# Parking weights in DRAM later, and counting their buffers by their last reader, in an attention + two-FFN kernel on one core

## The chip, the cores and the metric

One NeuronCore of a Trainium2 chip runs the whole program. The metric is the device time of one execution in microseconds; the figure for the kernel before is the median of three runs.

## The reference

Causal local/strided attention (4 batches, 8 heads, 576 positions, head size 64), then a gated feed-forward layer behind an RMS norm, then a second one without a norm. There are 2304 tokens, the model width is 512 and the hidden width 1536; all data are float32.

```python
attn = softmax(where(mask, q @ k.T / 8, -1e9))            # heads 0-3: local 32, heads 4-7: same position mod 32
x = (attn @ v).transpose(0, 2, 1, 3).reshape(2304, 512)
x = x / sqrt(mean(x * x) + 1e-6) * rms_g                  # first layer only
for w_gate, w_val, w_out in (layer1, layer2):
    g = x @ w_gate
    x = (g * sigmoid(g) * (x @ w_val)) @ w_out
```

## The kernel before, in words

**Arithmetic.** Each float32 operand is split in a high and a low part, and each product is made of three TensorE products (high·high, high·low, low·high). A weight comes from DRAM as words into a `raw` buffer (512 KB, `fetch`, L218). `scale` rebuilds it into `dh` in four operations: two on ScalarE (`low` L235, `high` L227), two on VectorE (`sign` L239, `join` L244). Then ScalarE casts the high part and VectorE subtracts it for the low part.

**Stages.** The hidden width is cut into 12 chunks of 128 columns per layer. Chunks 0 to 5 of the first layer are multiplied while attention still runs, in six token segments (`segs`, numbers 0 to 5) with `gate` and `down`. All other chunks go through the Strassen stage: 15 items (`work`), five passes of three token blocks of 768. The passes hold chunks (6, 7, 8) and (9, 10, 11) of the first layer, and (0..3), (4..7), (8..11) of the second. A chunk is seven products (steps 1 to 7) on `xq`, sums of quarters of x. GpSimd makes those: `sum_x` (L1165, on x fetched by `stage_x`, L1159) and the low parts `xl` in `split_q` (L1182). The next item's x is split while this item's last chunk is multiplied. `first_x` (L1064 to L1081) does the same for item 0 during segment 5, into the pool `x7`.

**Weights of the Strassen stage.** `combined_step` turns gate and value weight into seven quarter sums. Its operations in order: two loads, 4 + 4 of `scale`, one `sums` (four GpSimd subtractions, L326, VectorE's results in, VectorE's next inputs out), then a cast (L358) and a subtraction (L362) for each of four pieces. With "keep" (c) the pieces land in rooms of SBUF. With "park" (p) they overwrite `raw` and `dh`, and after each piece `save` stores the two halves to DRAM (`pk`, L370 and L371); `recall_step` (r, L397) later loads the four pieces into rooms with no arithmetic. `weight_step` (d) does a w_out chunk. Rooms: 20 of 4 KB and 5 of 2 KB per partition; a chunk of the Strassen stage takes 3 + 1, and one for w_out. A pass gives its rooms back chunk by chunk in its third item (`used`).

**The planner.** `plan` writes the order of these steps by hand into `late`. `point()` is called at fixed places between TensorE's products; each call advances `clock` by one, loads the next step of `late` if it is `ready`, and adds `pace["op"]` to an allowance from which operations of the steps begun are emitted. A step waits `state["wait"]` points after its load, and `state["lag"]` points before the operation marked `late`. `need_w` emits whatever is missing at a chunk's first use. A count `free` of raw buffers per rack (`racks[0]`) lets a step load: three in the pool `dec`, which also holds the x of the segments (`load_x`, L865), and five in the pool `st`. `st` is opened when attention is closed (L1107) and taken down at the start of segment 5, after `while begun: operate(begun[0])`.

**Order on the engines.** Each engine runs its queue in order, and the order is fixed at build time by priority: an instruction's place in the program, less an offset (`PRIO` 200 for path operations, `PRIO_W` -150 for the weights). `behind(eng)` puts a weight operation after the last path operation of its engine. All DMAs but two are issued by SyncE.

The lines that the change sits on, as they read before:

```python
            cell["bk"]["free"] += free                       # join: buffer counted free at once
        pace["op"] = 2.0                                     # segments
        state["lag"], state["wait"] = 10 if n else 5, 9      # items
            if z == 5 and nxt:
                cell = stage_x(nxt[0], nxt[2])
            if i == 0 and nxt:
                sum_x(cell)
```

Of the kernel before, what the change touches and what calls it, by code (L numbers as in the profile page):

```python
# [25 lines left out]
def attn_ffn_ffn(ctx: ExitStack, tc: tile.TileContext, q, k, v, w1g, w1v, w1o, rms_g, w2g, w2v, w2o, out):  # L26
# [117 lines left out]
    def weights():  # L144
        clock[0] += 1
        prefetch()
        have["op"] = min(have["op"] + pace["op"], 3.0)
        while have["op"] >= 1.0:
            fit = [st for st in begun if clock[0] - st.at >= st.lag]
            if not fit:  # L150
                break
            have["op"] -= 1.0
            operate(fit[0])
# [50 lines left out]

    rack = {"pool": dec, "free": 3, "bufs": 3, "dh": 2}
    racks = [rack]
    parked = {}
# [14 lines left out]
    def scale(cell, free=1):  # L222

        def high():
            cell["h"] = cell["bk"]["pool"].tile([128, 512], F32, tag="dh", name="dh", bufs=cell["bk"]["dh"])
            with behind("act"):
                nc.scalar.activation(out=cell["h"], in_=cell["hw"].bitcast(F32), func=AF.Copy, scale=2.0 ** -112)  # L227

        def low():
            cell["r"] = cell["lw"]  # L230
            if spare:
                spare.append(spare.pop(0))
                cell["r"] = pp.tile([128, 512], U32, tag=spare[-1], name="lws")
            with behind("act"):
                nc.scalar.activation(out=cell["r"], in_=cell["lw"], func=AF.Copy, scale=LOW)  # L235

        def sign():
            with behind("dve"):
                nc.vector.scalar_tensor_tensor(out=cell["r"], in0=cell["hw"], scalar=0x80000000, in1=cell["r"], op0=ALU.bitwise_and, op1=ALU.bitwise_or)  # L239

        def join():
            h = cell["h"].bitcast(U32)
            with behind("dve"):
                nc.vector.scalar_tensor_tensor(out=h, in0=h, scalar=3, in1=cell["r"], op0=ALU.logical_shift_left, op1=ALU.bitwise_or)  # L244
            cell["bk"]["free"] += free

        return [low, high, sign, join]

# [8 lines left out]
    def weight_step(m, c, z, park=False):  # L257
# [11 lines left out]
        def second():  # L269
            lo(cell["t"], cell["h"])  # L270
            wt[m, c, z] = cell["t"]
            wdone.add((m, c, z))
# [15 lines left out]
        def save():  # L288
            h, a = parts()
            d = dp.tile([128, 2, 512], F32, name=f"pk{m}_{c}")  # L290
            nc.sync.dma_start(out=d[:, 0], in_=h.bitcast(F32))
            nc.sync.dma_start(out=d[:, 1], in_=a)
            cell["bk"]["free"] += 1
            parked[m, c, z] = d

        return Step([load] + scale(cell, int(not park)) + ([high, low, save] if park else [first, second]),
                    lambda: (park or room[4]) and racks[0]["free"] >= 1, PRIO_W)

    QUARTERS = ((1, 2), (5, 6), (7, 4), (3,))

    def combined_step(m, c, how):
# [7 lines left out]
        def ready():  # L309
            if racks[0]["free"] < 2:  # L310
                return False
            return how == "park" or len(room[4]) >= n4 and len(room[2]) >= 7 - 2 * n4

# [6 lines left out]
        def sums():  # L320
# [3 lines left out]
            b12, b22 = v["h"][:, 0:256], v["h"][:, 256:512]  # L324
            for z, a, b in ((0, b12, b11), (2, b22, b12), (1, b22, t[:, 0]), (3, b21, t[:, 1])):
                nc.gpsimd.tensor_tensor(out=t[:, z], in0=a, in1=b, op=ALU.subtract)  # L326
            spaces = v["raw"].rearrange("p k f -> p (k f)").bitcast(F32)
# [16 lines left out]
        def op(i, f):  # L344
            def g_():
                f(*parts[i])
                if i == len(parts) - 1 and f is (save if how == "park" else second):
                    g["bk"]["free"] += 1
                    if how == "park":
                        v["bk"]["free"] += 1  # L350
                    else:
# [647 lines left out]
    def plan(text):  # L999
        for word in text.split():  # L1000
# [10 lines left out]

    plan("p19 p110 c16 d16 c17 c18 d17 d18 r19 d19 r110 d110 p111 p20 r111 d111 p21 r20 d20 r21 d21 p22 p23 r22 d22 r23 d23 "
         "c24 d24 p25 p26 p27 r25 d25 r26 d26 r27 d27 c28 d28 p29 p210 p211 r29 d29 r210 d210 r211 d211")
# [81 lines left out]
    for si, (m, t0, n, c0, c1) in enumerate(segs):  # L1095
# [10 lines left out]
        pace["dec"] = 0.25  # L1106
        pace["op"] = 2.0  # L1107
        xs = xs_of.pop(si)
        state["tanh"] = True and att is not None
        for c in range(c0, c1):  # L1110
# [6 lines left out]
            if att and not steps and not active_att():  # L1117
# [5 lines left out]
                open_pool("st", "st", 0, bufs=1)  # L1123
                racks.insert(0, {"pool": pools["st"][0], "free": 5, "bufs": 5, "dh": 5})
                room[4] += [(pools["wpb"][0], f"v{i}") for i in range(2)]
# [217 lines left out]
    for n, (m, cs, t0) in enumerate(work):  # L1343
# [51 lines left out]
        pace["op"] = 0.6 if n else 1.0  # L1395
        state["lag"], state["wait"] = 10 if n else 5, 9
        for z in (1, 0, 0, 2, 6, 0, 5, 7, 0):
            step(chunks[0], z) if z else blank()
            if z == 5 and nxt:
                cell = stage_x(nxt[0], nxt[2])  # L1400
            if z == 2:
                spare[:] = ya[halves[0].n:]
        for i, c in enumerate(chunks[:-1]):
# [6 lines left out]
            step(c1, 2)  # L1410
            if i == 0 and nxt:
                sum_x(cell)
            if i == k - 2:
                pace["op"] = 0.6 if n else 0.8
            step(c1, 6)
            blank()
# [59 lines left out]
```

## Time and profile before

| | us |
|---|---|
| median of 3 runs (lowest to highest) | 1059.54 (1057.32 to 1061.37) |
| the profiled execution's own time | 1058.73 |
| its span, first to last instruction | 1056.9 |
| TensorE busy / idle in the span | 992.2 / 64.7 |
| VectorE, ScalarE, GpSimd busy | 589.0, 575.5, 472.9 |
| DMA moved | 181.60 MB |
| mean granted TensorE clock (1.00 is full) | 0.964 |

Time runs from the span's start. A view of windows gives, for each stretch, its length, each engine's busy time with the number of instructions in brackets, the granted TensorE clock, the busy share of the DMA engines and what they moved. A row of waits names the engine and line that waited, what released it, and the total, the number of times and the longest, in us.

### The profile page before, as it was taken

The page shows a single profiled execution, that of the slowest core. Times are in us where ns is not written, and L with a number is a line of the kernel's source. Part 1 is how long each engine was busy: PE and PEld are TensorE (multiplying, and loading weights), DVE is VectorE, ACT ScalarE, POOL GpSimd, SP SyncE. Part 2 cuts the span into 40 slices and gives each one's busy share as a digit, 9 for nine tenths or more (in the row PEclk, how much of TensorE's full clock was granted, in tenths as well). Part 3 has the DMA queues.
Part 4 walks back from the last instruction along what each step waited for, and adds up shares of the span by engine and source line. Part 5 has one row for each costly group of instructions (what it writes and reads, how often), then busy time and mean ns, then how long its engine had stood idle before and what let it go on. Part 6 is the DMA issues. An engine that isn't in the chain of part 4 may idle for free. (4 is left out here: it accounts for less than half of the span.)

```text
span 1056.9 us, 16819 instructions
## 1 busy us (share of the span) xinstructions
PE 992.2 (94%) x5804; PEld 905.4 (86%) x5804; DVE 589.0 (56%) x1289; ACT 575.5 (54%) x1435; POOL 472.9 (45%) x485
## 2 busy tenths in 40 slices
PE   5758979999999997999987999999999999999998
PEld 4647869878778986999987999999998999899997
DVE  3779546445434186764756666555547665633433
ACT  5878745636633355753663565656547455643431
POOL 3312212203100294675956865837557473745500
PEclk9758989999999998999999999999999999999999
DMA  7576445224105129677687595257862739815021
GB/s 196 157 221 182 146 135 161 66 65 127 40 26 185 53 89 348 203 251 243 209 256 246 201 343 181 92 188 255 285 237 75 254 126 349 269 64 180 30 80 60
DMA packets 153277, 181.60 MB, mean 172 GB/s; under 512 B 44132, under 2 KB 120364, under 8 KB 153192
## 3 DMA queue, kind: packets, MB, share of 16 engines
q1 hardware_dynamic: 153000, 180.25, 52.6%
q8 instruction: 46, 0.75, 0.3%
q14 instruction: 39, 0.32, 0.1%
q0 software_dynamic: 192, 0.28, 0.1%
HBM read 123.60 MB, written 56.89 MB: 171 GB/s over the span
## 5 line engine op out<-in xcount | busy, mean ns | idle before, releaser
L1182 POOL TENSOR_TENSOR xl<-xst,xh 128x384 fp32r<-128x384 f32 x168 | 185.6, 1136 | 70.9 <-PE b_a L66 42.8
L66 PE MATMUL b_y<-xh,w 128*128 128x384 f32 x700 | 188.6, 336 | 4.0 <-ACT t L1210 4.0
L66 PE MATMUL b_g<-xh,w 128*128 128x384 f32 (+2 forms) x496 | 150.8, 352 | 9.7 <-ACT xh L905 7.0
L66 PEld LDWEIGHTS b_y<-xh,w 128*128 128x128 f32 x700 | 127.6, 188 | 7.6 <-ACT t L1210 5.7
L66 PE MATMUL b_a<-xh,w 128*128 128x384 f32 (+2 forms) x460 | 126.3, 338 | 5.6 <-DVE t L1220 5.5
L66 PE MATMUL b_v<-xh,w 128*128 128x384 f32 (+2 forms) x432 | 129.7, 350 | 0.0
L66 PE MATMUL b_y<-hh,w 128*128 128x256 f32 (+2 forms) x432 | 119.1, 347 | 3.7 <-ACT hh L892 3.7
L66 PE MATMUL b_y<-xl,w 128*128 128x384 f32 x350 | 117.4, 335 | 0.0
L66 PEld LDWEIGHTS b_g<-xh,w 128*128 128x128 f32 x496 | 93.3, 196 | 16.4 <-ACT xh L905 7.2
L66 PEld LDWEIGHTS b_a<-xh,w 128*128 128x128 f32 x460 | 83.9, 189 | 9.6 <-DVE t L1220 6.0
L635 POOL TENSOR_TENSOR e<-e,rc 128x384 f32<-128x384 f32 (+3 forms) x40 | 38.3, 961 | 119.6 <-DVE rc L629 84.3
L1181 ACT CAST xh<-xst 128x384 fp32r<-128x384 f32 x168 | 80.2, 522 | 12.5 <-POOL xst L1165 12.4
L66 PEld LDWEIGHTS b_y<-hh,w 128*128 128x128 f32 x432 | 78.3, 191 | 10.1 <-ACT hh L892 4.0
L66 PEld LDWEIGHTS b_v<-xh,w 128*128 128x128 f32 x432 | 79.7, 192 | 6.7 <-issue 0.4
L66 PE MATMUL b_g<-xl,w 128*128 128x384 f32 (+2 forms) x248 | 85.4, 344 | 0.0
L66 PE MATMUL b_a<-xl,w 128*128 128x384 f32 (+2 forms) x230 | 77.6, 337 | 0.0
L66 PE MATMUL b_y<-hl,w 128*128 128x256 f32 (+2 forms) x216 | 73.8, 342 | 2.4 <-DVE hl L893 1.7
L1165 POOL TENSOR_TENSOR s<-xst 128x384 f32<-128x384 f32 x28 | 28.8, 1049 | 104.5 <-DMA xst<-y_d 71.8
L66 PE MATMUL b_v<-xl,w 128*128 128x384 f32 (+2 forms) x216 | 73.5, 340 | 0.0
L66 PEld LDWEIGHTS b_y<-xl,w 128*128 128x128 f32 x350 | 65.7, 188 | 1.8
L66 PE MATMUL b_y<-w,hh 128*128 128x512 f32 x216 | 67.1, 392 | 0.0
L618 ACT ACTIVATE e<-e,nb 128x96 f32<-128x96 f32 (+2 forms) x152 | 56.6, 376 | 19.2 <-DVE nb L609 19.2
(210 smaller groups left out, 2198.3 us busy)
## 6 DMA issues: line engine op xcount, KB each, us to landing
w<-pk SPq DMA_DIRECT2D x39, 512.0 KB
pk<-raw SPq DMA_DIRECT2D x65, 256.0 KB
xst<-y_d SPq DMA_DIRECT2D x18, 768.0 KB
raw<-in_moe_w_gate_dram SPq DMA_DIRECT2D x24, 512.0 KB
raw<-in_moe_w_val_dram SPq DMA_DIRECT2D x24, 512.0 KB
raw<-in_moe_w_out_dram SPq DMA_DIRECT2D x24, 512.0 KB
part<-ob SPq DMA_DIRECT2D x48, 256.0 KB
ob<-part SPq DMA_DIRECT2D x36, 256.0 KB
```

The source lines that it names most:

```text
L66: traced(nc.tensor.matmul(out_, a, b_, start=start, stop=stop, **how))
L618: r = nc.scalar.activation(out=e[:qn, i, :kn], in_=e[:qn, i, :kn], func=AF.Exp, bias=nb[:qn, i:i + 1], scale=-1.0, accum_out=sums[:qn, i:i ...
L635: eng.tensor_tensor(out=e[:qn, :nt, :kn], in0=e[:qn, :nt, :kn], in1=rc[:qn, :nt].unsqueeze(2).to_broadcast([qn, nt, kn]), op=ALU.mult)
L1165: eng.tensor_tensor(out=out_[:, kk], in0=a[:, kk], in1=b[:, kk], op=op)
L1181: nc.scalar.copy(out=xh[:, kk], in_=src[:, kk])
L1182: eng.tensor_tensor(out=xl[:, kk], in0=src[:, kk], in1=xh[:, kk].bitcast(F32), op=ALU.subtract)
```

## The change

Parks start only once attention is over (`att is None`). The plan parks chunk 6 too and recalls it; chunk 11 of the first layer and chunks 0 and 1 of the second are no longer parked but split straight from their load, so 11 combined weights are parked in place of 13. A `raw` buffer is counted free six points after its last reader is emitted (`back`); each rack also counts its `dh` buffers (`words`, `spent`), and `high` (`cell`) is emitted only if one is free. `sums` is emitted with a priority offset of 200. `pace["op"]` is 2.5 in the segments before the last and 1.5 in the last; lag and wait become 6 and 6 in a segment that begins after attention, and 10 (8 in item 0) and 12 in the items. `stage_x` is emitted behind step 1 of an item's first chunk in place of step 5, and `sum_x` in loop k - 3 (the same loop for k = 3, one later for k = 4).

```diff
-            fit = [st for st in begun if clock[0] - st.at >= st.lag]
+            fit = [st for st in begun if clock[0] - st.at >= st.lag and (not hasattr(st[0], "cell") or words(st[0].cell["bk"]) > 0)]
...
-    rack = {"pool": dec, "free": 3, "bufs": 3, "dh": 2}
-    racks = [rack]
+    racks = [{"pool": dec, "free": 3, "bufs": 3, "dh": 2, "back": [], "words": 2, "wback": []}]
+
+    def back(bk, n):
+        bk["back"].append((clock[0] + 6, n))
+
+    def words(bk):
+        while bk["wback"] and bk["wback"][0] <= clock[0]:
+            bk["words"] += 1
+            bk["wback"].pop(0)
+        return bk["words"]
+
+    def spent(bk, n):
+        bk["wback"].append(clock[0] + n)
+        bk["wback"].sort()
+
+    def spaces():
+        bk = racks[0]
+        while bk["back"] and bk["back"][0][0] <= clock[0]:
+            bk["free"] += bk["back"].pop(0)[1]
+        return bk["free"]
...
         def high():
+            cell["bk"]["words"] -= 1
...
-            cell["bk"]["free"] += free
-
+            back(cell["bk"], free)
+
+        high.cell = cell
...
             lo(cell["t"], cell["h"])
+            spent(cell["bk"], 4)
...
-            cell["bk"]["free"] += 1
+            back(cell["bk"], 1)
+            spent(cell["bk"], 6)
...
-            if racks[0]["free"] < 2:
+            if spaces() < 2:
                 return False
-            return how == "park" or len(room[4]) >= n4 and len(room[2]) >= 7 - 2 * n4
+            return how == "park" and att is None or how != "park" and len(room[4]) >= n4 and len(room[2]) >= 7 - 2 * n4
...
-            for z, a, b in ((0, b12, b11), (2, b22, b12), (1, b22, t[:, 0]), (3, b21, t[:, 1])):
-                nc.gpsimd.tensor_tensor(out=t[:, z], in0=a, in1=b, op=ALU.subtract)
+            with tc.high_priority(offset=PRIO):
+                for z, a, b in ((0, b12, b11), (2, b22, b12), (1, b22, t[:, 0]), (3, b21, t[:, 1])):
+                    nc.gpsimd.tensor_tensor(out=t[:, z], in0=a, in1=b, op=ALU.subtract)
...
                 f(*parts[i])
+                if f is (save if how == "park" else second) and parts[i][0][0] in (1, 3):
+                    spent((g if parts[i][0][0] == 1 else v)["bk"], 6 if how == "park" else 8)
                 if i == len(parts) - 1 and f is (save if how == "park" else second):
-                    g["bk"]["free"] += 1
+                    back(g["bk"], 1)
                     if how == "park":
-                        v["bk"]["free"] += 1
+                        back(v["bk"], 1)
...
-    plan("p19 p110 c16 d16 c17 c18 d17 d18 r19 d19 r110 d110 p111 p20 r111 d111 p21 r20 d20 r21 d21 p22 p23 r22 d22 r23 d23 "
+    plan("p16 p19 p110 r16 d16 c17 c18 d17 d18 p22 r19 d19 r110 d110 p23 c111 d111 c20 d20 c21 d21 r22 d22 r23 d23 "
          "c24 d24 p25 p26 p27 r25 d25 r26 d26 r27 d27 c28 d28 p29 p210 p211 r29 d29 r210 d210 r211 d211")
...
-        pace["op"] = 2.0
+        pace["op"] = 2.5 if si < NA - 1 else 1.5
+        state["lag"], state["wait"] = (6, 6) if att is None else (3, 4)
...
-        state["lag"], state["wait"] = 10 if n else 5, 9
+        state["lag"], state["wait"] = 10 if n else 8, 12
         for z in (1, 0, 0, 2, 6, 0, 5, 7, 0):
             step(chunks[0], z) if z else blank()
-            if z == 5 and nxt:
+            if z == 1 and nxt:
                 cell = stage_x(nxt[0], nxt[2])
...
-            if i == 0 and nxt:
-                sum_x(cell)
             if i == k - 2:
                 pace["op"] = 0.6 if n else 0.8
+            if i == k - 3 and nxt:
+                sum_x(cell)
```

## Rows read from the trace of the kernel before

**Rows 1.** The page's 40 slices of the span: TensorE's busy tenths.
```profile
PE   5758979999999997999987999999999999999998
```

**Rows 2.** Windows of 5 us in the attention stage.
```profile
120.00:125.00 5.00, 2.87 (x18) 2.61 (x18) 2.82 (x14) 4.14 (x15) 0.26 (x1) 0.72 0.47 166
...
130.00:135.00 5.00, 1.93 (x18) 1.42 (x14) 4.50 (x12) 4.59 (x16) 4.04 (x5) 1.00 0.24 79
135.00:140.00 5.00, 1.03 (x3) 0.86 (x4) 2.33 (x8) 1.33 (x3) 0.78 (x1) 0.58 0.96 310
140.00:145.00 5.00, 5.00 (x44) 4.77 (x43) 1.84 (x4) 1.65 (x4) 0.00 (x0) 0.73 0.53 178
```

**Rows 3.** What ScalarE waited for, 100 to 145 us.
```profile
ACT xh L905 <- DMA xraw<-x_d: 3.9, 1, 3.9
ACT raw L358 <- DMA pk<-raw: 3.6, 1, 3.6
```

**Rows 4.** Timeline of SyncE's queue, 130 to 145 us (start, us, what).
```profile
134.07 0.38 SPq L865 DMA_DIRECT2D xraw<-x_d  x1
```

**Rows 5.** Windows of 5 us from the end of segment 5 on.
```profile
405.00:410.00 5.00, 1.98 (x11) 1.49 (x9) 1.49 (x3) 1.65 (x4) 4.84 (x6) 0.89 1.03 410
410.00:415.00 5.00, 2.67 (x6) 1.78 (x7) 4.97 (x7) 2.86 (x6) 1.92 (x2) 0.50 0.85 283
415.00:420.00 5.00, 5.00 (x17) 4.32 (x16) 3.58 (x6) 3.46 (x7) 0.00 (x0) 0.59 0.96 346
...
535.00:540.00 5.00, 2.08 (x12) 1.76 (x11) 0.65 (x1) 1.03 (x2) 3.87 (x4) 1.00 0.77 237
575.00:580.00 5.00, 0.45 (x3) 0.13 (x1) 1.03 (x1) 0.47 (x1) 3.68 (x5) 0.96 0.52 177
580.00:585.00 5.00, 4.04 (x13) 4.05 (x14) 3.15 (x7) 1.41 (x3) 3.31 (x3) 0.50 0.28 105
585.00:590.00 5.00, 5.00 (x27) 5.00 (x26) 2.78 (x4) 3.82 (x10) 3.18 (x3) 0.86 0.41 143
```

**Rows 6.** Waits of all engines, 405 to 420 us.
```profile
ACT raw L235 <- DMA raw<-in_moe_w_out_dram: 3.9, 1, 3.9
PE b_y L66 <- ACT hh L892: 3.7, 1, 3.7
```

**Rows 7.** Waits of all engines, 535 to 540 us.
```profile
ACT dh L227 <- DMA pk<-dh: 5.0, 1, 5.0
```

**Rows 8.** Waits of all engines, 565 to 590 us.
```profile
DVE dh L362 <- POOL raw L326: 8.3, 1, 8.3
POOL s L1165 <- DMA xst<-x_d: 6.6, 1, 6.6
```

**Rows 9.** Windows: segment 4, and segment 5.
```profile
326.00:357.00 31.00, 31.00 (x228) 29.60 (x227) 9.79 (x20) 10.01 (x20) 0.00 (x0) 1.00 0.36 117
357.00:405.00 48.00, 48.00 (x224) 40.20 (x223) 31.86 (x38) 26.59 (x52) 36.35 (x32) 1.00 0.41 130
```

**Rows 10.** Instruction groups by line (busy us, mean ns, idle before them).
```profile
L244 DVE SCALAR_TENSOR_TENSOR dh<-dh,raw 128x512 uint32<-128x512 uint32 x53 | 51.0, 963 | 10.7 <-ACT dh L227 9.7
L239 DVE SCALAR_TENSOR_TENSOR raw<-raw 128x512 uint32<-128x512 uint32 x53 | 47.5, 898 | 21.9 <-ACT raw L235 21.6
...
L362 DVE TENSOR_TENSOR raw<-raw 128x512 fp32r<-128x512 f32 x26 | 22.2, 858 | 8.8 <-ACT raw L358 8.6
...
L244 DVE SCALAR_TENSOR_TENSOR dh<-dh,lws 128x512 uint32<-128x512 uint32 x19 | 13.0, 684 | 1.0 <-ACT dh L227 0.4
...
L326 POOL TENSOR_TENSOR raw<-dh 128x256 f32<-128x256 f32 x36 | 28.5, 814 | 74.2 <-DVE dh L244 42.7 <-ACT b_v L1216 21.0 <-ACT w L358 7.5
```

**Rows 11.** The chain that ended last (start, us, what): two like places.
```profile
723.78 1.36 PE b_y L66 x6
...
816.08 1.36 PE b_y L66 x6
```

**Rows 12.** Waits of all engines, whole span.
```profile
POOL raw L326 <- DVE dh L244: 42.7, 10, 8.2
```

More of the change, by code (lines that the diff above doesn't have):

```diff
@@ L292, in save @@
             nc.sync.dma_start(out=d[:, 1], in_=a)
-            cell["bk"]["free"] += 1
+            back(cell["bk"], 1)
+            spent(cell["bk"], 6)
             parked[m, c, z] = d
         return Step([load] + scale(cell, int(not park)) + ([high, low, save] if park else [first, second]),
-                    lambda: (park or room[4]) and racks[0]["free"] >= 1, PRIO_W)
+                    lambda: (park or room[4]) and spaces() >= 1, PRIO_W)
     QUARTERS = ((1, 2), (5, 6), (7, 4), (3,))
@@ L1123, in attn_ffn_ffn @@
                 open_pool("st", "st", 0, bufs=1)
-                racks.insert(0, {"pool": pools["st"][0], "free": 5, "bufs": 5, "dh": 5})
+                racks.insert(0, {"pool": pools["st"][0], "free": 5, "bufs": 5, "dh": 5, "back": [], "words": 5, "wback": []})
                 room[4] += [(pools["wpb"][0], f"v{i}") for i in range(2)]
```

## The prediction

> **What bounds the kernel now.** The slices of the page come first: TensorE is full in nearly all slices, with thin ones up to slice 6 and dips around slices 16 and 22 [rows 1]. The kernel is bound by TensorE's queue, so a change gains only what it gives back in those dips. In a stretch I take as lost its length minus TensorE's busy time times the granted clock; that counts the idle time and also the half-speed matmuls behind it (clock 0.50 against 1.00, of the two levels 1.2 and 2.4 GHz). Then the windows, in steps of 5 us, and for each dip the chain of waits behind it.
>
> Dip 1, attention, 120 to 145 us without the full step 125 to 130: 5 - 2.87 x 0.72 = 2.9, then 3.1, 4.4 and 1.4, together 11.8 us [rows 2]. Two waits make it, both on the two parks that run here. ScalarE stood 3.6 us in a park's split until a store out of `raw` had landed, and 3.9 us in the cast of the next x until its load had landed [rows 3]. That load was issued only at 134.07, because it takes one of the three `raw` buffers of `dec` and the parks held them [rows 4].
>
> Dip 2, the door to the Strassen stage, 405 to 420: 3.2 + 3.7 + 2.0 = 9.0 us [rows 5]. ScalarE stood 3.9 us at the head of a w_out word that had not landed; queued behind it was `hh` (L892), for which TensorE waited [rows 6].
>
> Dip 3, 535 to 540: 2.9 us [rows 5]. ScalarE stood 5.0 us before writing a `dh` buffer from which a parked half was still being stored [rows 7].
>
> Dip 4, 575 to 590: 4.6 + 3.0 + 0.7 = 8.3 us [rows 5]. GpSimd waited 6.6 us for the next x with the rest of a combined step's `sums` behind it; VectorE waited 8.3 us for those sums, with the Strassen adds behind it [rows 8].
>
> Sum: 11.8 + 9.0 + 2.9 + 8.3 = 32.0 us.
>
> **The change part by part.** *Parks only after attention.* `late[0]` is a park, so nothing of the plan starts before attention is closed. p19 and p110 leave the attention stretch with their 4 weight loads, 16 stores, 16 ScalarE, 16 VectorE and 8 GpSimd operations; no park holds a `raw` buffer there, and the loads of x that queued behind the stores go out when emitted. Gain: between 0 (if attention's own chain were the limit) and 11.8 us. I take 11.8, since both waits end on a transfer of a park or behind one [rows 3, 4]. It is kept afterwards, as the following slices are full [rows 1] and x and attention are both emitted in TensorE's order.
>
> *Three parks (p16, p19, p110) in segment 4.* Now the five-buffer pool `st` is used, which stood empty in the old plan: its next steps needed rooms that only segment 5 frees. From 326 to 357 us TensorE is full and GpSimd idle [rows 9]. I count the points in the code: segment 4 has 36. A park waits 6 points, runs 12 operations at 2.5 a point, waits 6 and runs 9: 21 points. The second fits in the gaps of the first; the third starts when their buffers return, at about point 26, and `while begun` drains its last operations at the start of segment 5. VectorE per park: 2 x (0.898 + 0.963) + 4 x 0.858 = 7.2 us [rows 10], three 21.5; with the 9.79 already there 31.3 of 31.0 us [rows 9]. It just fits, and `hh` and `hl` of a chunk are wanted only two chunks later. Bounds: 0, and 21.5 us if nothing of it were hidden. I take 0, as VectorE's idle 21.2 us are nearer to the whole of it. Each park loads 1.0 MB and stores 1.8 (shapes): 8.4 MB in 31 us. With the 117 GB/s now shown that makes 388 GB/s [rows 9], against 410 that the queue moved in one step of dip 2 [rows 5]. If the cover goes, first_x is late: `x7` reuses the memory of `st`, so its first write waits for the last store. GpSimd is busy 36.35 of 48 us there [rows 9], which leaves 11.7 us before the first Strassen product waits.
>
> One rule speaks against this part. The row first: `join` on VectorE takes 0.963 us with both inputs in SBUF and 0.684 with one in PSUM [rows 10]. The Trainium skill, "SBUF — State Buffer", section "SBUF: two separate sides", says that a VectorE operation with two SBUF inputs and a GpSimd operation hold one port pair in turn, the later blocked until the earlier has ended; the rows agree in direction. By it the sum would be 10 us higher (rival B), by the row's own means, which already hold such meetings, nothing.
>
> *Chunk 6 recalled, longer waits before segment 5's splits.* r16 brings chunk 6 back without a single ScalarE or VectorE operation, so segment 5 splits two chunks in place of three, and the time from load to first use grows from 4 to 6 points there, about 1 us each (50 points in 48 us [rows 9]), then to 12 in the first Strassen item. The late word of dip 2 landed 3.9 us after ScalarE stood ready; 2 to 3 points more and a DMA queue without r19's recall just there should cover it. Gain: 0 to 9.0; I take 9.0.
>
> *`dh` counted free behind the store* (`words`, `spent`: 6 to 8 points after a park's store is emitted) removes the wait of dip 3 by definition of the count, if 6 points exceed a store's landing. Points there come every 0.64 us: two four-chunk items take 816.08 - 723.78 = 92.3 us [rows 11], so 46 us and 72 points each. That is 3.8 us, against the 5.0 that ScalarE stood. Gain 0 to 2.9; I take half of it, 1.5.
>
> *Sums ahead of the x work on GpSimd, x sooner.* `sums` gets priority over `sum_x`, and `stage_x` is emitted after product 1 in place of 5, so the sums no longer stand behind a landing x. `sum_x` itself moves one chunk later in four-chunk items, still two chunks before its result is split. Gain 0 to 8.3; I take 8.3. Late next: the x low parts, if a sum waits for VectorE (rival C).
>
> *Fewer parks, later buffers.* 11 weights go out and return in place of 13: 7.2 MB less, hidden, so nothing. `back` holds a `raw` 6 points longer and `wait` grows by 3, so a park cycle in the four-chunk items goes from 54 to 63 points. Counted through the calls of `point`, the last parks still come in time: chunk 11 of the second layer is recalled at point 14 of its pass and first used at about 49, 35 points or 22 us later; c111, now split straight from its load, ends 20 points before its use. No `need_w` is forced. Cost 0; if the cover were gone, 9 points or 5.8 us per park.
>
> Sum of gains: 11.8 + 9.0 + 1.5 + 8.3 = 30.6 us. Against it I put one new stall of the size of dip 3, 2.9 us, as every in-order queue is dealt anew in the stage that had three. 1058.7 of the profiled execution - 30.6 + 2.9 = 1031.0; the median of the runs lies 0.8 above that execution: 1031.8, so 1032.
>
> **The rivals.** A: only attention gains. Dips 2 to 4 are fixed orders meeting late transfers, and new ones of the same size appear elsewhere: 1059.5 - 11.8 = 1048. For it: three dips of three different releasers [rows 6 to 8]. Against: each has its own remedy here.
>
> B: the parks fill VectorE in segment 4. Twelve sums of 0.81 us on GpSimd [rows 10], each holding up a VectorE operation, add 9.8 us to 31.3 of 31.0; TensorE waits 10 us: 1042. For it: the 0.963 against 0.684. Against: the means already hold part of it, and segment 5 can take a remainder. (This is the Trainium skill's rule cited above.)
>
> C, the other side: the sums are now ahead of the x low parts, and wait at GpSimd's head for VectorE. They did so 10 times for 42.7 us, 4.3 each, 8.2 at most [rows 12], when their priority was low. The Strassen stage has 13 such steps; if each holds the next item's x up so far that TensorE loses 4.3 us, that is 56 us: 1088. It turns the result to slower from (30.6 - 2.9 + 5.3) / 13 = 2.5 us per step. Against: sums of other steps than dip 4's never stopped TensorE.
>
> D: nothing lands. Attention's next chain takes the place of the x load, and the late dips move: 1059. Against: in each dip the last releaser is something that the change moves [rows 3, 6 to 8].
>
> **How the numbers follow.** Forecast 0.50 (own range 1025 to 1040), A 0.26, B 0.09, C 0.07, D 0.08. Predicted is the forecast's 1032. With A and B 0.85 are held; low end all of the 32.0 gained plus the spread of the runs (2 us), 1059.5 - 32.0 - 2 = 1025, and 3 us for small waits in the same slices that I did not add: 1022; high end A with that spread: 1050. Faster by over 0.5% (5.3 us, about what a measurement of this kernel can tell): forecast, A and B, 0.85. Same: D, 0.08. Slower: C, 0.07.
>
> **What would show it.** Right: no stores to `pk` before attention ends; TensorE busy over 4.8 of each 5 us from 120 to 145 at clock 1.00; no ScalarE wait above 2 us on a w_out load at the end of segment 5; none on a store from `dh`; the sums of a step back to back on GpSimd, none behind `s` (L1165). Wrong: TensorE idle in segment 4 or at its end, or waiting on GpSimd's low parts at an item's start; a recall that lands after its chunk's first use.

## The result, and the profile after

The changed kernel is slower: 1069.71 us (median of 5 runs, 1064.77 to 1073.45) against 1059.79 for the kernel before in the same measurement, a ratio of 1.0095 (95% interval 1.0066 to 1.0125). Forecast was 1032. Two executions, one of the kernel before (3357 us) and one of an experiment below (3036 us), are left out of the medians and ratios. Line numbers are 20 to 27 higher in the changed kernel: the words' `raw` operations L235 and L239 are now L255 and L259, `dh` L227 is L247, `join` L244 is L264, `sums` L326 is L350, `s` L1165 is L1192, `xh` and `xl` of `split_q` are L1208 and L1209, `hh` L892 is L918. L1237 and L1247 copy and add the Strassen products, L1251 is the SiLU of the gate, L276 the low part of a w_out weight.

The slices of the page after answer to [rows 1]: the dips of slices 6 and 22 are gone, but new ones stand in slices 18 and 20.

```profile
PE   4758999999999998979899999999999999999998
```

Windows after, as in [rows 2]. Dip 1 is gone, at full clock:

```profile
120.00:125.00 5.00, 5.00 (x48) 4.72 (x47) 1.92 (x12) 2.75 (x13) 0.83 (x1) 1.00 0.03 10
...
130.00:135.00 5.00, 5.00 (x53) 4.72 (x52) 2.66 (x11) 3.14 (x10) 0.51 (x1) 1.00 0.37 118
135.00:140.00 5.00, 5.00 (x64) 4.68 (x63) 0.42 (x1) 1.80 (x5) 0.00 (x0) 1.00 0.01 4
140.00:145.00 5.00, 5.00 (x57) 4.60 (x56) 3.24 (x7) 3.62 (x11) 0.00 (x0) 1.00 0.32 105
```

Windows after at the door to the Strassen stage (395 to 415 is what 405 to 420 was in [rows 5]), in the first item, and at dip 4:

```profile
395.00:400.00 5.00, 2.50 (x11) 1.74 (x11) 2.98 (x5) 3.88 (x7) 0.30 (x1) 1.00 0.86 258
400.00:405.00 5.00, 4.64 (x23) 3.87 (x22) 3.12 (x6) 2.18 (x6) 2.06 (x2) 1.00 0.98 330
405.00:410.00 5.00, 3.42 (x18) 3.10 (x18) 2.14 (x2) 2.15 (x6) 4.92 (x7) 1.00 0.93 276
410.00:415.00 5.00, 2.96 (x10) 2.96 (x11) 3.37 (x6) 3.11 (x7) 0.34 (x1) 0.73 0.93 333
...
465.00:470.00 5.00, 3.52 (x18) 3.03 (x18) 3.42 (x4) 4.62 (x11) 3.93 (x5) 1.00 0.82 265
470.00:475.00 5.00, 1.38 (x7) 1.05 (x7) 4.90 (x6) 3.43 (x8) 5.00 (x4) 0.87 0.01 3
475.00:480.00 5.00, 5.00 (x16) 5.00 (x17) 3.46 (x6) 2.93 (x7) 5.00 (x7) 0.50 0.14 52
...
585.00:590.00 5.00, 1.65 (x8) 1.23 (x8) 3.80 (x7) 4.28 (x10) 2.98 (x4) 0.98 0.01 3
590.00:595.00 5.00, 5.00 (x21) 5.00 (x22) 3.61 (x4) 3.30 (x8) 5.00 (x5) 0.68 0.66 197
```

By the prediction's way of counting, the door loses 2.5 + 0.4 + 1.6 + 2.8 = 7.3 us in these windows and 1.0 in the next three (9.0 before, and nothing in the next two), dip 4 3.4 + 1.6 = 5.0 (8.3 before), and the first item 1.5 + 3.8 + 2.5 = 7.8 us between 465 and 480. The kernel before loses nothing in these, while the next x is split there too:

```profile
465.00:470.00 5.00, 5.00 (x31) 5.00 (x30) 2.12 (x5) 2.62 (x6) 3.11 (x4) 1.00 1.02 376
470.00:475.00 5.00, 5.00 (x31) 5.00 (x30) 2.82 (x5) 3.75 (x10) 4.92 (x5) 1.00 0.32 91
475.00:480.00 5.00, 5.00 (x31) 5.00 (x29) 3.20 (x6) 3.59 (x9) 5.00 (x7) 1.00 0.61 180
```

Both kernels issue the same 5804 matmuls in the same order (only some weight buffers have other names), so the time from the Nth to the Mth matmul's start can be set side by side. This table is worked out from the matmul records of one profiled execution each, in us; "condition alone" and "with the list" are experiments below:

```
matmuls            before  condition alone  with the list  changed kernel
0 to 700            134.9       122.2           123.3          123.5
700 to 2300         229.4       230.2           229.4          229.2
2300 to 2400         22.7        22.7            22.7           23.7
2400 to 2700         64.6        63.3            74.0           66.7
2700 to 2800         17.3        17.3            17.3           25.4
2800 to 3000         34.7        34.8            34.7           39.1
3000 to 3600        116.6       116.1           113.7          115.1
3600 to 4600        191.2       191.3           191.7          194.3
4600 to 5200        115.8       116.0           116.3          121.4
5200 to 5803        116.5       116.5           116.5          116.5
```

Attention gains 11.4 us and keeps them up to the 2300th matmul; from there to the end the Strassen stage gives back 22.9. Attention's 700 matmuls took 120.8 to 128.8 us in the other profiles of kernels that do not park there, so its gain carries some 4 us either way. 24 executions of the kernel before on one chip went from 1053.8 to 1068.0 us, so a difference of a few us between two profiles can be that of two executions.

### The profile page after: what moved, and what is told of

Same layout as the page of the kernel before. It is cut to its first block, busy times and chain, and to the rows that moved or that the text cites. A ratio compares the mean times of both kernels' runs of the same rounds, so it can differ in the third digit from the quotient of the medians.

```text
span 1068.4 us, 16738 instructions
## 1 busy us (share of the span) xinstructions
PE 995.9 (93%) x5804; PEld 904.3 (85%) x5804; DVE 594.3 (56%) x1289; ACT 575.4 (54%) x1435; POOL 468.4 (44%) x485
## 4 chain that ended last, share of the span: by engine, by line
PE 63%; DMA 11%; POOL 9%; DVE 6%; ACT 6%; issue 4%; SPq 1%; DVEq 0%; POOLq 0%; ACTq 0%
PE b_y L66 26%; PE b_a L66 13%; PE b_g L66 12%; PE b_v L66 10%; POOL xl L1209 3%; DMA raw<-in_moe_w_gate_dram 3%; PE b_a L69 3%; POOL raw L350 2%; DMA raw<-in_moe_w_val_dram 2%; POOL xl L1107 1%; DMA xst<-x_d 1%; DMA pk<-raw 1%; POOL xst L1192 1%; DVE raw L259 1%; DVE dh L388 1%
## 5 line engine op out<-in xcount | busy, mean ns | idle before, releaser
L1209 POOL TENSOR_TENSOR xl<-xst,xh 128x384 fp32r<-128x384 f32 x168 | 181.6, 1113 | 104.5 <-PE b_a L66 32.2
L66 PE MATMUL b_y<-xh,w 128*128 128x384 f32 x700 | 191.0, 339 | 11.4 <-ACT t L1237 5.5
L1208 ACT CAST xh<-xst 128x384 fp32r<-128x384 f32 x168 | 80.1, 522 | 14.3 <-POOL xst L1192 14.2
L1192 POOL TENSOR_TENSOR s<-xst 128x384 f32<-128x384 f32 x28 | 29.1, 1059 | 123.5 <-DMA xst<-y_d 75.4
```

The lines of the kernel that those rows point to most:

```text
L66: traced(nc.tensor.matmul(out_, a, b_, start=start, stop=stop, **how))
L1192: eng.tensor_tensor(out=out_[:, kk], in0=a[:, kk], in1=b[:, kk], op=op)
L1208: nc.scalar.copy(out=xh[:, kk], in_=src[:, kk])
L1209: eng.tensor_tensor(out=xl[:, kk], in0=src[:, kk], in1=xh[:, kk].bitcast(F32), op=ALU.subtract)
```

## The experiments

Eighteen kernels, in three kinds: the changed kernel with one part undone, the kernel before with one part alone, and combinations. Each ratio is to the kernel before run on the same chip, and its interval is one of 95%. That kernel's median lay between 1060.7 and 1062.2 us there, so the ratios compare better than the times.

**Undoing one part of the change.** Old pace, lags and waits:

```diff
-        pace["op"] = 2.5 if si < NA - 1 else 1.5
-        state["lag"], state["wait"] = (6, 6) if att is None else (3, 4)
+        pace["op"] = 2.0
-        state["lag"], state["wait"] = 10 if n else 8, 12
+        state["lag"], state["wait"] = 10 if n else 5, 9
```

> The changed kernel with the old points: pace 2.0 in every stage of part A, lag 5 and wait 9 in the first Strassen item. Theory of the bunched splits: the new lags and waits hold the steps of the weights back, so that they come out together in the first item, beside the splitting of the last chunk of x (the changed kernel loses 8 us against the one before between 450 and 485 us). Undone, the first item gets that back: 1058 to 1062 us, the matmuls of the first item 8 to 10 us ahead of the changed kernel's, and no stall of the weights' ScalarE instructions at 465 to 480. Rivals: the counting of buffers or the GpSimd priority holds the steps back. Then this run stays at 1066 to 1073 us, with the same loss in the first item.

Measured: 1049.05 us, ratio 0.9866 (0.9820 to 0.9912), faster than expected. The first item's hundred matmuls (2700 to 2800) fall from 25.4 to 19.7 us, not to 17.3; the execution profiled was the slowest of the four (1055.8 us).

Old counting: `back(bk, n)` becomes `bk["free"] += n`, and `words` returns 1.

> The changed kernel with a buffer counted free at once behind its last reader's recording, as before, and the high words never waited for. Theory of the bunched splits by lag and wait: no part of the loss hangs on the counting, the time stays at 1066 to 1073 us. Rival, the counting: the delay of 6 points makes each step begin later, the steps pile up on the first items; undone, 1055 to 1062 us, with the first item's loss of 8 us gone. Should the counting be what keeps waits away, the time goes above 1074 us, with ScalarE's dh and raw waiting for stores in segments 4 and 5.

Measured: 1057.45 us, 0.9964 (0.9933 to 0.9996). The rival is right too: the counting has its share of the loss.

The sums at their old priority (`with tc.high_priority(offset=PRIO)` taken off):

> The changed kernel with the four sums of a split weight at their old priority on GpSimd, behind the low parts of x. Theory of the bunched splits by lag and wait: the sums' place is worth no more than 3 us either way, 1066 to 1073 us. Rival (the slower side of the forecast: sums ahead of the low parts of x on GpSimd hold up the matmuls that read these): undone, 1050 to 1060 us, and the stall of 9 us near 580 us, where the high words wait for the sums, goes back to what the kernel before shows there, 8 us.

Measured: 1065.64 us, 1.0048 (1.0013 to 1.0083). The interval overlaps the changed kernel's: a cost of the sums' place is not shown, and by the two ratios it is at most a small part (0.5%).

`stage_x` back at step 5 and `sum_x` back at `i == 0`:

> The changed kernel with the next x loaded and summed where the kernel before does it. The sums of x wait 4 to 14 us for their data in nearly every item of the changed kernel, as they did before, since the one x buffer is still being read when the load is issued. Theory: this part changes nothing, 1067 to 1073 us. Rival: the earlier load takes SP's queue from the stores and loads of the weights, and the later sums (third point from the end) come out among the weights' work; undone, the slow creep between 600 and 940 us (9 us in the changed kernel) goes away, 1060 to 1064 us.

Measured: 1064.09 us, 1.0017 (0.9985 to 1.0048), at the edge of what the rival had: in the changed kernel this part costs about 0.8%. In its profile the 4600th to 5200th matmul takes 116.0 us against 121.4.

The old list:

> The changed kernel with the old list of weights. If the new list is what the first item suffers from: 1048 to 1060 us, the first item's loss of 8 us gone. If lags and counting do it whatever the list: 1065 to 1075 us.

Measured: 1051.93 us, 0.9919 (0.9884 to 0.9954). The list has its share as well; of the first item's loss about half is left (58.0 us from the 2700th to the 3000th matmul, 64.5 in the changed kernel, 52.0 before).

The pace's two halves, first the items' lag and wait alone undone, then part A's pace alone:

> The changed kernel with the first Strassen item's lag and wait as before (5 and 9 in place of 8 and 12); the pace of part A stays new. Undoing both gave 20 us. If the first item's longer lag is what holds the steps back until they bunch beside the last chunk of x: 1049 to 1054 us. If the pace of part A (1.5 points where it was 2.0 once attention is over) leaves fewer steps done at the door to the Strassen stage: 1065 to 1071 us, no gain.

> The changed kernel with part A's pace, lag and wait as before (2.0, and the old lags); the first Strassen item's longer lag and wait stay. The mirror of the run beside it: if part A's pace is the cause, 1049 to 1054 us, and 33 to 34 of the 72 high words scaled by the 2500th matmul (30 in the changed kernel, 33 in the one before). If the first item's lag is: 1065 to 1071 us.

Measured: 1055.02 us, 0.9933 (0.9905 to 0.9960), and 1059.91 us, 0.9986 (0.9959 to 1.0013). Neither theory had it alone; both halves matter, but not in the same place. With part A's pace undone the hundred falls to 20.9 us. With the first item's lag and wait undone it stays at 24.7; the profile gains 6.5 us from the 3000th to the 3600th matmul (108.6) and 5.7 from the 4600th to the 5200th (115.7). So the theory that the first item's lag costs its time in the first item is not borne out. The second run's 31 high words at the 2500th matmul fell short of the 33 to 34 it was to show.

**One part alone.** The kernel before with one line changed:

```diff
-            return how == "park" or len(room[4]) >= n4 and len(room[2]) >= 7 - 2 * n4
+            return how == "park" and att is None or how != "park" and len(room[4]) >= n4 and len(room[2]) >= 7 - 2 * n4
```

> The kernel before with one condition alone changed: a split weight is parked only once attention is over. Theory of the added parts: the attention part's 11.5 us come from this condition by itself and nothing of the Strassen stage's 23 us of loss does, so 1059.5 - 11.5 = 1048 us (1045 to 1052). Rival: work parked later must be done later whatever the counting, and the Strassen stage gives it back: 1056 to 1062 us.

Measured: 1046.11 us, 0.9865 (0.9819 to 0.9911). The condition by itself is worth 1.35%, and the Strassen stage takes 678.0 us from the 2300th matmul on, against 679.3 before and 702.2 in the changed kernel. Postponing the parks costs nothing later that these profiles show.

That, and the whole new list; then only its first half (`p16 p19 p110 r16 d16` for `p19 p110 c16 d16`); then only the other (no `p16`, three fewer parked):

> The kernel before with that condition and the new list of weights (fewer parked, chunk 6 of the first weight matrix parked too). Theory: with the old lags, counting, priorities and loads the list costs nothing, 1045 to 1052 us as with the condition alone; less parking could give up to 5 us more where the stores of segment 5 no longer hold up the door to the Strassen stage (1043 us). Rival: the list itself puts more splitting into the first item, 1054 to 1062 us.

> The kernel before with parking only after attention, and the list changed at one place: chunk 6 of the first weight matrix is parked and loaded back. The condition alone gave 1046 us, with the whole new list 1055. If the parked chunk 6 costs the 9 us (one more combined weight to be split before the door): 1053 to 1057 us, the list's loss between the 2400th and 2700th matmul there. If the lesser parking does: 1044 to 1049 us.

> The kernel before with parking only after attention, and the new list but for chunk 6, which is kept as before: three combined weights (chunk 11 of the first matrix, chunks 0 and 1 of the second) are split directly in their places. If the lesser parking costs the 9 us (their sums and splits come in the Strassen items, with no slack there): 1053 to 1057 us. If chunk 6 does: 1044 to 1049 us, or up to 3 us less for the transfers saved.

Measured: 1055.25 us, 0.9950 (0.9921 to 0.9979); 1050.31 us, 0.9897 (0.9845 to 0.9950); 1050.00 us, 0.9866 (0.9823 to 0.9909). The list costs 0.85% of the time. By the ratios chunk 6 costs 0.3% and the lesser parking nothing, but neither half stands clear of the condition alone; the profiles show 5.5 and 3.5 us more from the 2300th matmul on (8.9 for the whole list). It arises at the door, from the 2400th to the 2700th matmul: 63.3 us, 69.4, 69.0, and 74.0. Waits of all engines from 384 to 456 us, with the condition alone and then with `p16` too:

```profile
ACT raw L235 <- DMA raw<-in_moe_w_out_dram: 3.1, 1, 3.1
PE b_y L66 <- ACT hh L892: 3.0, 1, 3.0
...
ACT w L358 <- POOL raw L326: 1.8, 1, 1.8
```

```profile
PE b_y L66 <- ACT hh L892: 6.2, 2, 5.7
...
ACT w L358 <- POOL raw L326: 4.2, 3, 2.3
...
ACT raw L235 <- DMA raw<-in_moe_w_out_dram: 2.4, 3, 1.3
```

ScalarE's wait for w_out words [rows 6] is a little shorter with `p16`, as forecast, but its waits at the head of a weight split for GpSimd's sums grow from 1.8 to 4.2 us, and TensorE's wait for `hh` doubles from 3.0 to 6.2.

The condition with the first item's longer lag and wait, and with shorter ones (3 and 7):

> The kernel before with parking only after attention, and of the rest of the change the first Strassen item's longer lag and wait alone (8 and 12 for 5 and 9). If late steps are the cost whatever else is there: 36 high words or fewer are scaled by the 2700th matmul (37 without the longer lag), a stall between the 2700th and the 3000th, 1050 to 1058 us. If the lag only costs together with the new list and the new counting: 1044 to 1048 us, the 17.3 us for these hundred matmuls kept.

> The same with the first item's lag and wait shortened instead (3 and 7 for 5 and 9), the dose in the other direction. If earlier is always better there: 1040 to 1044 us. If 5 and 9 already bring all steps out before the 2700th matmul, nothing is left to gain, and steps that come too soon meet the stores and loads at the door: 1046 to 1052 us.

Measured: 1052.71 us, 0.9910 (0.9885 to 0.9935), and 1052.25 us, 0.9907 (0.9878 to 0.9936). The longer lag gives about the time that was expected for a cost, but its interval overlaps the condition's own. Its profile has 1.8 us more in the hundred from the 2700th matmul, though all 37 words were scaled by then, so the count of words alone does not tell it. The shorter lag changes no step up to the 3000th matmul; its profile gains 4 us from the 3000th to the 3600th and loses 7 from the 4600th to the 5200th, in items whose lags were not touched, where a park's store stood at the head of SyncE's queue for 7.2 us, among other waits. This loss stays unexplained.

The condition with the sums' priority; with x's points; with both:

> The kernel before with parking only after attention, and the four sums of a split weight ahead of x's low parts on GpSimd. The forecast took 8.3 us of gain from this at 575 to 590 us (565 us in this version, VectorE's dh waits there 6.7 us for GpSimd's sums). If that stands by itself: 1038 to 1042 us. If the stall passes on (the same sums wait for data or buffers, or x's low parts are late instead): 1044 to 1050 us.

> The kernel before with parking only after attention, and x loaded sooner and summed later as in the change. If the later sums of x let the weight's four sums pass them: the stall near 565 us goes and 1040 to 1043 us. If the x buffer is read as long as before, so that x lands no sooner: 1044 to 1049 us, the stall moved by some us only.

> The same with the sums' priority as well. If the two parts need each other for the forecast gain of 8 us: 1036 to 1040 us and no stall over 3 us between 550 and 600 us. If neither does it: 1042 to 1048 us, as with the priority alone (1043.5).

Measured: 1043.50 us, 0.9835 (0.9811 to 0.9859); 1047.16, 0.9864 (0.9826 to 0.9902); 1049.08, 0.9857 (0.9813 to 0.9900). No interval stands clear of the condition's own, so neither part has a gain that was measured here. The first has the lowest ratio of all, 1.65% under the kernel before. But its dip 4 is there as before. GpSimd's timeline in it (`sums` is L327 here, `s` L1166):

```profile
554.74 1.43 POOL L327 TENSOR_TENSOR raw<-dh 128x256 f32<-128x256 f32 x2 [3.69 <-issue]
556.12 0.75 POOL L327 TENSOR_TENSOR raw<-dh,raw 128x256 f32<-128x256 f32 x1
562.99 1.94 POOL L1166 TENSOR_TENSOR s<-xst 128x384 f32<-128x384 f32 x2 [6.12 <-DMA xst<-x_d]
564.88 0.72 POOL L327 TENSOR_TENSOR raw<-dh,raw 128x256 f32<-128x256 f32 x1
```

Three of the four sums get ahead; the fourth still stands behind `s`, and `s` waits for x. VectorE waits 7.8 us for it, TensorE 5.0:

```profile
DVE dh L363 <- POOL raw L327: 7.8, 1, 7.8
POOL s L1166 <- DMA xst<-x_d: 6.1, 1, 6.1
...
PE b_a L66 <- DVE t L1221: 5.0, 1, 5.0
```

**Pairs undone.** The changed kernel without the new pace and counting, and without the new list and pace:

> The changed kernel with old pace, lags and waits, and old counting of buffers: the condition, the list, the sums' priority and the earlier x are left. By themselves these two undone gave 20 and 12 us. If both work by one mechanism (steps held back until they bunch in the first items), the sum is not reached: 1045 to 1050 us. If they are two costs that add: 1070 - 32 = 1038 us (1035 to 1042).

> The changed kernel with the old list and the old pace, lags and waits: the condition, the counting, the sums' priority and the earlier x are left. With the new list these three gave 6 us (1049 against 1055 us). If that holds with the old list too: 1038 to 1043 us, the fastest of all. If they only repair what the list does: 1044 to 1050 us, as with the condition alone.

Measured: 1054.14 us, 0.9927 (0.9902 to 0.9951), and 1054.98 us, 0.9943 (0.9919 to 0.9967). The parts do not add: neither pair undone is faster than the old pace alone (0.9866), and the second is slower clear of the noise. With the old pace the new counting gained some 5 us by the medians (the intervals just meet); with the new pace it cost 12.

**What they have in common.** ScalarE scales 72 high words (`dh` L227 / L247) and GpSimd makes 72 of these sums up to the end. Counting those done when the 2700th and the 2800th matmul start tells whether a weight's steps fall into this hundred, where the last chunk of item 0 is multiplied and the next x is split:

```
kernel                           high words     sums    us for the 100
before; condition alone; with    37 -> 37     28 -> 28   17.3 or 17.4
  either half of the list, all
  of it, sums, x, sums + x, the
  shorter lag; pace + counting
  undone (10 kernels)
condition + longer lag           37 -> 37     24 -> 28   19.1
list undone                      35 -> 35     20 -> 24   19.3
pace undone                      37 -> 37     24 -> 28   19.7
part A's pace undone             36 -> 37     24 -> 28   20.9
counting undone                  35 -> 37     24 -> 28   21.0
list + pace undone               35 -> 37     24 -> 26   22.1
first item's lag undone          34 -> 37     24 -> 26   24.7
sums undone                      33 -> 37     24 -> 24   24.7
x undone                         33 -> 37     24 -> 24   24.9
changed kernel                   33 -> 37     24 -> 24   25.4
```

The two ends of it as rows, ScalarE's L227 (before) and L247 (changed) counted from the start to the 2500th, 2700th and 2800th matmul (the second number in a row is their busy time, the count stands in brackets):

```profile
0.00:425.10 425.10, 21.60 (x33) 0.92 0.46 139
0.00:460.40 460.40, 24.62 (x37) 0.93 0.47 144
0.00:477.70 477.70, 24.62 (x37) 0.93 0.48 147
```

```profile
0.00:414.60 414.60, 20.04 (x30) 0.94 0.49 146
0.00:452.30 452.30, 22.04 (x33) 0.94 0.49 147
0.00:477.70 477.70, 24.67 (x37) 0.94 0.49 150
```

In ten kernels no step falls into this hundred and it takes what the matmuls take; in all ten others some do, and the more words, the longer. (In three of these only sums fall in.) The hundred is not the whole loss: the condition with the list, and pace + counting undone, keep 17.3 us there and still take 1054 to 1055; in their profiles the 2400th to the 2700th matmul take 74.0 and 77.1 us, against 64.6 before.

How a late step costs TensorE time is on VectorE's timeline of the changed kernel:

```profile
470.30 1.30 DVE L264 SCALAR_TENSOR_TENSOR dh<-dh,raw 128x512 uint32<-128x512 uint32 x1
471.53 1.50 DVE L276 TENSOR_TENSOR w<-dh,w 128x512 fp32r<-128x512 f32 x1
472.96 1.49 DVE L259 SCALAR_TENSOR_TENSOR raw<-raw 128x512 uint32<-128x512 uint32 x1
474.37 0.54 DVE L1247 TENSOR_TENSOR t<-t,b_y 128x384 f32<-128x384 f32 x1
```

and on TensorE's:

```profile
471.20 0.45 PE L66 MATMUL b_y<-xh,w 128*128 128x384 f32 x1 [1.91 <-ACT t L1237]
...
474.96 0.69 PE L66 MATMUL b_y<-xh,w 128*128 128x384 f32 x1 [2.42 <-DVE t L1247]
```

L1247 adds a Strassen product for the next matmul. Three weight operations of 1.30 to 1.50 us stand in front of it and TensorE waits 2.42 us; ScalarE's L1237 stands behind four weight operations and a cast of x, and TensorE waits 1.91. Then the clock is at 0.50 from 475 to 480 us, the lower of the two levels, so 16 matmuls run in 5 us. No run put the path's operations ahead of the same steps, so this reading of the timeline was not tested by an edit.

## Why the prediction was wrong

The table of matmuls sets the forecast beside the two profiles, before and after. Attention: a gain of 11.8 us forecast, 11.4 measured. The door (2300 to 2700): a gain of 9.0 forecast, a loss of 3.1 measured. Dips 3 and 4 (both between 3000 and 3600): a gain of 9.8 forecast, 1.5 measured. Everything else: a loss of 2.9 forecast; measured are losses of 12.5 from the 2700th to the 3000th matmul and of 8.7 behind the 3600th.

**Dip 1: right.** 11.8 us were forecast, 11.4 came in the profile, and the condition alone gave 1.35% (14 us by the medians). It was kept up to the end, so the condition by itself (1046) came out near where rival A had put the whole change, 1048.

**Three parks in segment 4 at no cost: right.** From the 700th to the 2300th matmul 229.4 us became 229.2. Rival B did not happen. Only the tail of the third park hung over: its last eight stores went out from the 2276th to the 2312th matmul, and the hundred from the 2300th took 1.0 us more.

**The step that failed: "Fewer parks, later buffers: cost 0".** It priced a longer wait and a later buffer only by whether a chunk's split ends before its first use; the first item's longer wait it counted, besides, as part of the gain at dip 2, and the slower pace of the last segment not at all. No wait of TensorE in the changed kernel's Strassen stage names a weight, so as far as the profile shows no chunk was late. The steps did not come too late for their matmuls; those seen at 470 to 475 us came while ScalarE and VectorE had their path operations to do, and stood in front of them. At the 2700th matmul 33 high words were scaled, four fewer than before, and the four came in the next hundred. In that hundred and the next two TensorE lost 8.1 + 4.4 us against before, about half of what the stage gave back. The list, part A's pace and the counting move steps this way: each undone alone gives 1.1 to 1.8% back and shortens the hundred (to 19.3, 20.9 and 21.0 us). The first item's lag and wait undone give 1.6% back, but behind the 3000th matmul, by a way that was not traced; pace, lag and wait together give 2.3%. None of these is needed for the attention gain, which the condition has alone. The prediction looked for this only as rival C's wait on GpSimd, or as "one new stall of 2.9 us"; the Strassen stage gave back 23 in all.

**Dip 2, forecast 9.0: not gained.** The windows at the door lost 8.3 us up to 430 in the changed kernel, and by the matmuls the door became 3.1 us longer. ScalarE's wait for w_out words went down from 3.9 to 2.2 us and TensorE's for `hh` from 3.7 to 2.3, so the mechanism was there, but TensorE also waited 1.75 us for a SiLU (L1251) and 2.22 for a copy of a Strassen product (L1237), both on ScalarE. With the list on top of the condition the door became 10.7 us longer. The new list was taken as less work; the runs showed that it costs time there; through which of its halves is not settled.

**Dip 3, forecast 1.5: right in the wait, not in the time.** ScalarE's wait of 5.0 us for a store out of `dh` [rows 7] is not among the waits from 526 to 560 us any more, but in them ScalarE waits 4.0 us for GpSimd's sums and TensorE 3.2 us, in three pieces, for ScalarE; by the prediction's way of counting 530 to 560 us lose 3.8 us, more than the 2.9 before:

```profile
ACT w L384 <- POOL raw L350: 4.0, 1, 4.0
...
PE b_y L66 <- ACT t L1237: 3.2, 3, 1.4
```

**Dip 4, forecast 8.3: about 3 of it by the windows (8.3 to 5.0), and not by the way described.** x lands no sooner: `s` waited 104.5 us in 14 cases before (71.8 and 32.7, for the two sources of x), 123.6 in 14 after. The waits of the whole span, after:

```profile
POOL s L1192 <- DMA xst<-y_d: 75.4, 9, 11.8
...
POOL s L1192 <- DMA xst<-x_d: 48.2, 5, 13.9
...
POOL raw L350 <- DVE dh L264: 29.7, 4, 13.8
```

An earlier place in the program does not load x earlier: in 13 of 14 items the load leaves SyncE's queue within 16 matmuls of where it left before, early or late (the 3465th before and the 3458th after, the 4132nd and the 4146th). That fits the one x buffer that `xl` still reads; a second buffer was not tried. The priority moves three sums of four. On top of the condition both parts alone and together left the stall at 6.2 to 7.8 us of VectorE's waiting (6.7 with the condition alone). In the changed kernel with the first item's lag and wait undone the stall is not there: the 3300th to the 3400th matmul take 17.4 us, against 25.6 before and 22.8 in the changed kernel, and the 3000th to the 3600th 8.0 less than before. So by that profile most of the 9.8 us forecast for dips 3 and 4 could be had; which order of steps gives it was not traced.

**Rival C, the slower side, is not the main cause.** GpSimd's sums waited less for VectorE than before, 29.7 us in place of 42.7 [rows 12], though once 13.8 us where the longest was 8.2; no wait of TensorE in the changed kernel names GpSimd's low parts of x, and undoing the priority gave back at most a small part.

**Open.** Of the 24.2 us between the changed kernel's Strassen stage and the condition's alone, the 2700th to 3000th matmul holds 12.4. The 3.4 from the 2400th to the 2700th, and the 8.4 behind the 3600th, were located but not explained. In the largest of these ScalarE waited 6.7 us on an output buffer of VectorE's (`ob`) and TensorE 2.2 on ScalarE:

```profile
ACT b_y L1243 <- DVE ob L1341: 6.7, 1, 6.7
...
PE b_y L66 <- ACT b_y L1243: 2.2, 1, 2.2
```

A like stall of 7 us appeared once with lags unchanged there, so part of it may come from the order that is dealt anew by any edit. Why the parts do not add is not settled either.

## What to carry to other kernels

Where helper work shares in-order engines with the path, its price depends on what stands beside it, not on its sum or its deadline: before lengthening a wait, count what is then emitted in each stretch and look at the slack of VectorE and ScalarE there. A change of many parts that moves a schedule should be taken apart early: here one condition was worth 14 us and all the rest cost more than that. And an earlier place in the program brings a load forward only if its buffer is free earlier.

## What the runs showed that was not expected

The same weight operation takes nearly twice as long when GpSimd works: L264 took 0.69 us at 466.14, while GpSimd was idle until 466.57, and 1.30 at 470.30, while GpSimd ran without a gap. GpSimd's own subtractions took 1.01 us at 464.49 and 1.44 to 1.46 then:

```profile
464.49 1.01 POOL L1192 TENSOR_TENSOR xst<-s,xst 128x384 f32<-128x384 f32 x1
466.57 2.11 POOL L1209 TENSOR_TENSOR xl<-xst,xh 128x384 fp32r<-128x384 f32 x2 [1.07 <-ACT xh L1208]
...
469.61 1.45 POOL L1209 TENSOR_TENSOR xl<-xst,xh 128x384 fp32r<-128x384 f32 x1
471.02 1.46 POOL L1192 TENSOR_TENSOR xst<-xst 128x384 f32<-128x384 f32 x1
472.45 1.44 POOL L1209 TENSOR_TENSOR xl<-xst,xh 128x384 fp32r<-128x384 f32 x1
```

```profile
466.14 0.69 DVE L264 SCALAR_TENSOR_TENSOR dh<-dh,raw 128x512 uint32<-128x512 uint32 x1
```

The Trainium skill, "SBUF — State Buffer", section "SBUF: two separate sides", says that such a pair of operations takes turns at one port pair. The direction agrees; in the profile both sides are longer, VectorE's by 0.6 and GpSimd's by 0.44 us. It shows over the whole kernel before: of the 53 joins with both inputs in SBUF (L244) the 25 with no GpSimd operation beside them took 0.69 us each, as much as those with one input in PSUM, and the 20 with GpSimd busy from start to end 1.24 on average. The mean of 0.963 [rows 10], which the prediction went by, mixes the two. So a weight step is dearest just where x is being summed and split, which is where the change put those of four words.
